# One tile shape per TensorE visit, constants as late tasks and a reorder moved from the vector engine to Pool, in a fused attention and MLP kernel

## The chip, the cores and the metric

One Trainium2 chip, one core. The metric is the device time of one execution in microseconds; a time that is quoted is the median of several executions. Engine names in the profile: PE is TensorE's matmuls, PEld its weight loads, DVE the vector engine, ACT the scalar engine, POOL is GpSimd, SP issues transfers. With one core there is no second die to compare with. The kernel before took 390.67 us (390.64 to 390.71, 3 runs). Kernels are compared only within the same rounds.

## The reference

```python
B, H, S, D = 8, 8, 576, 64                      # q, k, v: float32
q_d, k_d, v_d = (x.reshape(B, H, 144, 4, D).mean(axis=3) for x in (q, k, v))
out_up = repeat(softmax(q_d @ k_d.T / 8) @ v_d, 4)         # pooled attention, 144 x 144
mask = abs(pos[:, None] - pos[None, :]) < 4                # a narrow band
out_local = softmax(where(mask, q @ k.T / 8, -1e9)) @ v    # local attention
x = (out_up + out_local).transpose(0, 2, 1, 3).reshape(4608, 512)
h = x @ w_in                                    # 512 -> 2048
out = (h * sigmoid(h)) @ w_out                  # 2048 -> 512
```

The 64 heads are handled as 32 pairs, and two pairs make a quad (16 of them). The MLP needs x for 512 tokens at a time, so its matmuls can run from about 50 us on, between those of attention.

## The kernel before

It is one program for all engines. Tasks (a cast, a mask product, a PV visit) are put in order at build time by a scheduler that plays through estimated durations, named `cost` in nanoseconds; each engine then has its own list in that order, with waits on semaphores. A block of matmuls that TensorE runs for one task is called a visit here: S2 makes the last scores and the pooled ones, Z the row sums of the softmax, PV the product with v. The parts that the change touches (cut):

```python
def order_T(s, x):                    # q and k come back from a DMA transpose in another order
    src = (qr if x == "q" else kr)[:, :, 64 * h:64 * h + 64].rearrange("p r g -> p g r")
    dst = (qT if x == "q" else kT)[y][:, :].rearrange("p (g r) -> p g r", r=9)
    if x == "q":
        P.op("DVE", lambda e: e.tensor_reduce(dst, src.unsqueeze(3), mybir.AxisListType.X, ALU.add),
             r=[R("qr")], w=[R(f"qT{y}")], cost=745)
    else:
        P.op("ACT", lambda e: e.activation(dst, src, AF.Copy), ...)

def castv(i):                         # v summed in fours, for two pairs, on Pool; 3 buffers vd
    t = vq[0:112, :, :, 0:128]
    pool(lambda g: g.tensor_tensor(t, t, z, ALU.add), ...)
    pool(lambda g: g.tensor_tensor(vd[m][0:112, ...], x, y, ALU.add), ...)

def ph_S2(p):                         # last scores, then pooled scores: 12 matmuls of 72 columns
    ...
    for i in range(3):
        for b in range(2):
            for h in range(2):
                rows = slice(64 * h, 64 * h + 64)
                mm(D[rows, b, 120 + 72 * i:192 + 72 * i], kd[j][rows, i:i + 190:3],
                   qd[j][rows, 72 * b:72 * b + 72], ..., m="diag")

def do_mask(p):                       # DVE, both inputs in SBUF
    P.op("DVE", lambda e: e.tensor_tensor(Pt[m][:, :, :], Pt[m][:, :, :],
         mask_bf[:, :].unsqueeze(1).to_broadcast([128, 2, S_]), ALU.mult), ..., cost=800)

def ph_Z(z):                          # row sums: 32 matmuls of 128 rows, then 24 of 48 rows
    ...
        mm(D[o:o + 32, 0, 0:72], onesZ[64 * a:64 * a + 48, 8 + c // 3, :],
           Pd[m][64 * a:64 * a + 48, c // 3, c % 3, :], ..., m="diag4")

def ph_PV(p):                         # 10 matmuls of 128 rows, then 6 of 48 rows
    ...
    rows = slice(64 * a, 64 * a + 48)
    for i3 in range(3):
        for h in range(2):
            mm(D[64 * h:64 * h + 64, 1, 120:264], vd[nd][rows, i3, h, :], Pd[ms[h]][rows, :, i3, :], ..., m="diag")
```

About thirty memsets for constants stand at the head of the vector engine's list (`const_id`).

The softmax here doesn't subtract the row's maximum and nothing guards it: scores larger than these inputs give would overflow.

## Time and profile before

| what | before |
|---|---|
| median time | 390.67 us |
| TensorE busy, idle (of a span of 389.2 us) | 354.7, 34.5 us |
| TensorE idle in 0-60, 60-100, 100-260, 260-360 us | 20.3, 3.8, 6.3, 0.8 us |
| DVE, ACT, Pool busy | 239.6, 215.1, 136.9 us |

Idle time is the length of a stretch less TensorE's busy time in it. The page's line on busy time (engine, busy us, share of the span, instructions):

```profile
PE 354.7 (91%) x3841; PEld 221.3 (57%) x3880; DVE 239.6 (62%) x394; ACT 215.1 (55%) x364; POOL 136.9 (35%) x173
```

TensorE is busy nine tenths of the span; the DVE, at 62%, has room on average.

### The profile page before, as it was taken

What the parts mean: (1) busy time and instruction counts of PE and PEld (TensorE: products, weight loads), DVE (VectorE), ACT (ScalarE), POOL (GpSimd) and SP (SyncE); (2) the same over time, 40 slices, a digit from 0 to 9 for tenths busy, and PEclk for the clock granted to TensorE, in tenths of its full rate; (3) what the DMA queues carried; (4) which work ended last, traced back from release to release, by engine and by line L of the source; (5) the groups of instructions that cost most, each with busy time, mean ns of one, the idle gap of its engine ahead of it and who ended that gap; (6) DMA issues with size and microseconds to landing.
All of it is one profiled execution on the core that took longest, in us unless ns stands there. A gap on an engine that the chain in (4) does not pass through costs nothing.

```text
span 389.2 us, 9061 instructions
## 1 busy us (share of the span) xinstructions
PE 354.7 (91%) x3841; PEld 221.3 (57%) x3880; DVE 239.6 (62%) x394; ACT 215.1 (55%) x364; POOL 136.9 (35%) x173
## 2 busy tenths in 40 slices
PE   0768599898999999999699999999999999999996
PEld 0656476655655556556455655666555656556542
DVE  6927477779978775986558899654363433334310
ACT  4756367666656765786167768463424344344321
POOL 7746826377624533452534622550040000000000
PEclk9968699999999999999879999999999999999999
DMA  8998997699999999999999999964000101101012
GB/s 260 323 319 232 177 250 191 193 250 240 262 247 274 194 252 242 285 219 220 173 256 239 195 174 226 211 156 108 27 29 32 51 27 44 39 27 53 29 54 81
DMA packets 87464, 66.77 MB, mean 172 GB/s; under 512 B 65152, under 2 KB 67200, under 8 KB 87424
## 3 DMA queue, kind: packets, MB, share of 16 engines
q1 hardware_dynamic: 83200, 59.90, 66.1%
q0 software_dynamic: 4224, 6.29, 7.3%
q8 instruction: 30, 0.49, 0.6%
q14 instruction: 10, 0.08, 0.1%
HBM read 53.67 MB, written 9.88 MB: 163 GB/s over the span
## 4 chain that ended last, share of the span: by engine, by line
PE 76%; DVE 15%; DMA 5%; issue 3%; ACT 1%; DVEq 0%; ACTq 0%
PE hps L481 31%; PE ops L481 30%; PE duo L481 12%; DMA qr<-qb 5%; DVE qd L519 3%; DVE qT L388 3%; DVE gT L754 2%; DVE qT L499 2%; DVE Pt L556 2%; PE duo L491 1%; DVE kd L519 1%; PE ops L491 0%; DVE rr L577 0%; DVE osb L308 0%; DVE duo L655 0%
## 5 line engine op out<-in xcount | busy, mean ns | idle before, releaser
L481 PE MATMUL hps<-xT,w_in_sb 128*128 128x512 f32 x544 | 169.9, 437 | 4.1 <-DVE gT L754 3.9
L754 DVE SCALAR_TENSOR_TENSOR gT<-th,hps 128x512 bf16<-128x512 f32 x136 | 92.5, 682 | 87.6 <-ACT th L752 87.5
L481 PE MATMUL ops<-w_out_bf,gT 128*128 128x512 bf16 x537 | 137.6, 383 | 3.9 <-issue 2.4
L752 ACT ACTIVATE th<-hps 128x512 f32<-128x512 f32 x136 | 81.2, 598 | 107.5 <-PE hps L481 107.3
L481 PEld LDWEIGHTS hps<-xT,w_in_sb 128*128 128x128 f32 x544 | 101.3, 193 | 34.5 <-DVE gT L754 7.1
L481 PEld LDWEIGHTS ops<-w_out_bf,gT 128*128 128x128 bf16 x576 | 47.5, 98 | 68.3 <-issue 25.5
L731 POOL TENSOR_TENSOR xT<-xo 128x576 fp32r<-128x576 f32 (+2 forms) x40 | 39.9, 1018 | 73.1 <-DVE xo L714 73.0
L433 POOL TENSOR_TENSOR vq<-vq 112x768 f32<-112x768 f32 x12 | 22.4, 1868 | 37.4 <-DMA vq<-in_v_dram 37.4
L556 DVE TENSOR_TENSOR Pt<-Pt,mask_bf 128x1152 bf16<-128x1152 bf16 x32 | 28.1, 884 | 11.8 <-ACT Pt L548 11.7
L775 ACT ACTIVATE osb<-ops 128x512 f32<-128x512 f32 x36 | 21.5, 597 | 25.1 <-PE ops L481 24.9
L532 ACT ACTIVATE Pt<-duo 128x912 bf16<-128x912 f32 x28 | 26.0, 928 | 6.4 <-PE duo L481 6.3
L519 DVE TENSOR_REDUCE qd<-qT 128x144 bf16<-128x576 bf16 x32 | 24.1, 752 | 5.7 <-PE duo L481 4.5
L422 POOL CAST qb<-qs 128x576 bf16<-128x576 f32 x27 | 18.8, 705 | 22.9 <-PE duo L491 17.8
L427 ACT ACTIVATE vb<-vs 128x640 bf16<-128x640 f32 x30 | 21.8, 738 | 4.0 <-DMA vs<-in_v_dram 2.4
L422 POOL CAST kb<-ks 128x576 bf16<-128x576 f32 x27 | 18.8, 708 | 8.4 <-DMA kr<-kb 6.6
L711 DVE TENSOR_TENSOR xo<-duo,Rb 128x456 f32<-128x456 f32 x29 | 18.0, 628 | 5.0 <-PE duo L481 2.9
L388 DVE TENSOR_REDUCE qT<-qr 128x576 bf16<-128x576 bf16 x16 | 18.6, 1162 | 3.4 <-DMA qr<-qb 3.4
L519 DVE TENSOR_REDUCE kd<-kT 128x144 bf16<-128x576 bf16 x26 | 18.9, 741 | 1.3 <-ACT kT L391 1.3
L391 ACT ACTIVATE kT<-kr 128x576 bf16<-128x576 bf16 x16 | 19.1, 1221 | 0.1
L550 ACT ACTIVATE Pd<-duo 128x432 bf16<-128x432 f32 x30 | 16.0, 534 | 0.0
L481 PE MATMUL duo<-qd,kd 64*64 64x72 bf16 x360 | 14.2, 218 | 0.8 <-DVE kd L519 0.8
L481 PEld LDWEIGHTS duo<-qT,kT 64*128 64x128 bf16 x284 | 8.1, 95 | 11.9 <-issue 6.3
(119 smaller groups left out, 297.6 us busy)
## 6 DMA issues: line engine op xcount, KB each, us to landing
vs<-in_v_dram SPq DMA_DIRECT2D x60, 160.0 KB, 5.2
out_dram<-osb SPq DMA_DIRECT2D x36, 256.0 KB, 2.0
Rb<-scr SPq DMA_DIRECT2D x24, 360.0 KB, 6.8
qs<-in_q_dram SPq DMA_DIRECT2D x29, 288.0 KB, 6.2
ks<-in_k_dram SPq DMA_DIRECT2D x29, 288.0 KB, 6.2
vq<-in_v_dram SPq DMA_DIRECT2D x24, 288.0 KB, 6.3
w_in_sb<-in_moe_w_in_dram POOLq DMA_DIRECT2D x4, 1024.0 KB, 8.2
w_out_bf<-in_moe_w_out_dram POOLq DMA_DIRECT2D x4, 512.0 KB, 10.4
```

What stands on the lines that cost most here:

```text
L388: P.op("DVE", lambda e: e.tensor_reduce(dst, src.unsqueeze(3), mybir.AxisListType.X, ALU.add), r=[R("qr")], w=[R(f"qT{y}")], cost=745)
L422: pool(lambda g: g.tensor_copy(dst, t), r=rs_, w=w, cost=650)
L427: P.op("ACT", lambda e: e.activation(vb[m][:, :, :], t, AF.Copy), r=rs_, w=[R(f"vb{m}")], cost=730)
L433: pool(lambda g: g.tensor_tensor(t, t, z, ALU.add), r=[R("vq"), R("vqz")], w=[R("vq")], cost=1900)
L481: return P.op("PE", lambda t: t.matmul(out_, lhsT, rhs, start=start, stop=stop, skip_group_check=True), r, w, cost=cost)
L519: P.op("DVE", lambda e: e.tensor_reduce(dst[j][:, 0:144], src[y][:, :].rearrange("p (g r) -> p g r", r=4), mybir.AxisListType.X, ALU.add), ...
L532: later("ACT", f"e1{p}", [(lambda e: e.activation(Pt[m][:, :, 0:456], D[:, :, 0:456], AF.Exp, scale=0.125), bk, [R(f"P{m}")], 930)], bk)
L556: P.op("DVE", lambda e: e.tensor_tensor(Pt[m][:, :, :], Pt[m][:, :, :], mask_bf[:, :].unsqueeze(1).to_broadcast([128, 2, S_]), ALU.mult), ...
L731: P.op("POOL", lambda e, dst=dst, in0=in0, in1=in1: e.tensor_tensor(dst, in0, in1, ALU.add), r=[R(f"xo{x}")], w=xblk(kc, t, e_), cost=200 ...
L752: later("ACT", f"th{n}", [(lambda e: e.activation(th[tb][:, :], hp, AF.Tanh, scale=0.5), [hr], [R(f"th{tb}")], 597)], [hr], pre=[f"st{n - ...
L754: later("DVE", f"st{n}", [(lambda e: e.scalar_tensor_tensor(gT[j % 2][:, f, :], th[tb][:, :], 1.0, hp, ALU.add, ALU.mult), [hr, R(f"th{tb} ...
L775: later("ACT", f"ob{n}", [(lambda e: e.activation(osb[s_][:, :], ops[:, ob, :], AF.Copy, scale=0.5), [R(f"o{ob}", True)], [R(f"osb{s_}")], ...
```

## The change

The intent: within a visit, matmuls on 48 rows follow matmuls on 128 rows, and each such change of tile shape costs time: in the trace of the kernel before, 146 ns from the last pair of one shape to the first of the next in PV, where full-height pairs follow each other every 49 ns, and 128 ns in Z, where single matmuls follow every 8 on average. So the v means and the sum weights are padded with zeros to 128 rows (PV, Z). The pooled scores use 144 columns where they can (S2). The constants become tasks that may run late. The q reorder goes from the DVE to Pool. To feed the padded v means, half of the second v sum goes from Pool to the DVE (`castv1`). Quad 7 gets its q and k through the DMA transpose too. Some estimated durations are mended, and the order of all tasks is searched anew. The core of the diff (cut):

```diff
-        vd = sb("vd", [128, 3, 2, 64], BF16, NVD)             # NVD = 3
+        vd = sb("vd", [128, 2, 3, 2, 64], BF16, NVD)          # NVD = 2, zero outside its rows
...
             if x == "q":
-                P.op("DVE", lambda e: e.tensor_reduce(dst, src.unsqueeze(3), mybir.AxisListType.X, ALU.add),
-                     r=[R("qr")], w=[R(f"qT{y}")], cost=745)
+                pool(lambda e: e.tensor_copy(dst, src), r=[R("qr")], w=[R(f"qT{y}")], cost=700)
...
-            pool(lambda g: g.tensor_tensor(vd[m][0:112, :, :, :].rearrange("p i h d -> p h i d"), x, y, ALU.add),
-                 r=[R("vq")], w=[R(f"vd{m}")], cost=1100)
+            pool(lambda g: g.tensor_tensor(
+                vd[m][0:48, 0, :, :, :].rearrange("p i h d -> p h i d"), x[0:48], y[0:48], ALU.add), ..., cost=1030)
+
+        def castv1(i):
+            x, y = (vq[64:112, :, :, lo:lo + 64] for lo in (0, 64))
+            P.op("DVE", lambda e: e.tensor_tensor(
+                vd[m][64:112, 1, :, :, :].rearrange("p i h d -> p h i d"), x, y, ALU.add), ..., cost=480)
...
-            for i in range(3):
-                for b in range(2):
-                    for h in range(2):
-                        mm(D[rows, b, 120 + 72 * i:192 + 72 * i], kd[j][rows, i:i + 190:3], qd[j][rows, 72 * b:72 * b + 72], ...
+            for i, b, lo, hi in ((0, 0, 0, 144), (1, 1, 0, 144), (2, 0, 0, 72), (2, 1, 72, 144)):
+                for h in range(2):
+                        mm(D[rows, b, x:x + hi - lo], kd[j][rows, i:i + 190:3], qd[j][rows, lo:hi], ...
...
-                    mm(D[o:o + 32, 0, 0:72], onesZ[64 * a:64 * a + 48, 8 + c // 3, :], ..., m="diag4")
+                    mm(D[o:o + 32, 0, 0:72], onesZ[:, 8 + 2 * a + y, :], rhs, ..., m="col4")
...
-                    mm(D[64 * h:64 * h + 64, 1, 120:264], vd[nd][rows, i3, h, :], Pd[ms[h]][rows, :, i3, :], ..., m="diag")
+                    mm(D[64 * h:64 * h + 64, 1, 120:264], vd[nd][:, a, i3, h, :], t[:, i3, 0:144] ..., m="col")
...
-        const_sel()                                            # and some thirty memsets at the head of the DVE's list
+        task("DVE", "c.ones", [], const_ones)                  # likewise c.dm, c.pad, c.vd
```

## The prediction

> **What bounds the kernel now.** I read the page first (busy shares, slices, chain), then the stretches table, then the timeline of single visits on TensorE. The page:
>
> ```profile
> PE   0768599898999999999699999999999999999996
> DVE  6927477779978775986558899654363433334310
> PEclk9968699999999999999879999999999999999999
> DMA  8998997699999999999999999964000101101012
> PE 76%; DVE 15%; DMA 5%; issue 3%; ACT 1%; DVEq 0%; ACTq 0%
> ```
>
> A slice is 9.7 us. TensorE (PE) is at nine tenths or more from slice 8 on, with one hole in slice 19. Loading keeps the DMA engines full for about 25 slices, then only the MLP is left, at the full rate of PE. The chain that ended last is three quarters PE. The stretches (columns: stretch, its us, then busy us of PE, PEld, DVE, ACT, POOL, granted clock, DMA share, GB/s):
>
> ```profile
> 0.00:60.00 60.00, 39.73 (x860) 31.70 (x862) 38.28 (x90) 33.98 (x60) 37.01 (x68) 0.86 1.03 261
> 60.00:100.00 40.00, 36.15 (x547) 24.02 (x550) 32.93 (x49) 27.99 (x52) 23.79 (x27) 1.00 0.85 223
> 100.00:180.00 80.00, 77.91 (x970) 47.03 (x977) 63.82 (x99) 53.32 (x89) 34.37 (x41) 1.00 1.09 247
> 180.00:200.00 20.00, 16.78 (x151) 10.06 (x149) 11.03 (x16) 10.13 (x17) 8.63 (x9) 0.83 1.26 181
> 200.00:260.00 60.00, 59.00 (x682) 36.30 (x690) 47.05 (x74) 41.31 (x68) 27.84 (x27) 1.00 1.03 213
> 260.00:360.00 100.00, 99.21 (x537) 59.21 (x546) 41.58 (x64) 40.56 (x69) 5.24 (x5) 1.00 0.13 44
> ```
>
> PE idles 20.3 us in the first 60 us (8.85 of it before its first matmul), 3.9 in the next 40, 6.3 in 100 to 260, and 0.8 of 100 after that. DMA saturation does not bind the end: at 260 us, when loading is over, about 100 us of MLP still wait for PE, so PE always has a backlog and every microsecond of PE time removed after some 60 us should leave the total. The DVE (63.8 of 80 us in the middle) is the runner-up.
>
> **Where PE loses time.** One attention visit after another in the timeline, clock 1.00:
>
> ```profile
> 153.18 0.44 PE L481 MATMUL duo<-Pt,vb 128*64 128x120 bf16 x10
> 153.86 0.44 PE L481 MATMUL duo<-Pt,vb 128*64 128x120 bf16 x10
> 154.54 1.20 PE L481 MATMUL hps<-xT,w_in_sb 128*128 128x512 f32 x4
> ...
> 155.67 0.58 PE L481 MATMUL duo<-qT,kT 64*128 64x120 bf16 x10
> 156.18 0.46 PE L481 MATMUL duo<-qd,kd 64*64 64x72 bf16 x12
> ```
>
> A PV visit takes 0.68 us from start to start. The starts of its single records give the parts: the ten full-height matmuls go in pairs every 49 ns, the six 48-row ones of 144 columns every 60 ns, so streaming is 5 x 49 + 3 x 60 = 425 ns. The other 255 ns are two changes of tile shape: from the last pair of one shape to the first of the next it is 146 to 152 ns instead of 49 to 60, and the first pair after it is followed 25 to 27 ns late. One change costs about 0.12 us.
>
> [...] In S2 the pooled scores reload the same weights for every 72 columns: 253 ns between the first and last of 12 starts, 23 ns each or 46 a pair, against 30 ns by columns (a 144-column pair takes 60). [...] Here the DVE's reordering reduce takes 1162 ns, Pool's cast of as many elements 705:
>
> ```profile
> L388 DVE TENSOR_REDUCE qT<-qr 128x576 bf16<-128x576 bf16 x16 | 18.6, 1162 | 3.4 <-DMA qr<-qb 3.4
> L422 POOL CAST qb<-qs 128x576 bf16<-128x576 f32 x27 | 18.8, 705 | 22.9 <-PE duo L491 17.8
> ```
>
> **The change part by part.**
> 1. PV in one shape: 32 visits lose their inner change, 32 x 0.12 = 3.8 us. Where two PV follow each other directly (9 times after 60 us, some 11 in all), the change between them goes too: 11 x 0.12 = 1.3 us. Sum 5.1 us. Streaming stays 60 ns a pair.
> 2. Z in one shape: 12 visits, 128 ns instead of 8 at the boundary: 12 x 0.12 = 1.4 us. Its 56 matmuls keep their 8 ns each.
> 3. S2: the change from scores to pooled scores stays (142 ns), but 12 matmuls become 4 of 144 columns and 4 of 72. Pairs: 2 x 60 + 2 x 46 = 212 ns, before 6 x 46 = 276. 32 x 0.064 = 2.0 us.
> 4. Quad 7 goes from PE transposes to the DMA transpose: two visits of nine less, each about 0.51 us (457 ns between first and last start, plus one step): 1.0 us. It adds two transposes to a full DMA, hidden if they are issued in time.
> So PE work falls by 5.1 + 1.4 + 2.0 + 1.0 = 9.5 us. Of the 1 to 3 parts, 26 of 32 PV and S2 visits and all Z lie after 60 us: about 26 x 0.12 + 9 x 0.12 + 1.4 + 26 x 0.064 = 7.3, plus the 1.0 makes 8.3 us on the path. The rest falls in a stretch where PE waits anyway; I count none of it.
> 5. Constants as late tasks. PE starts at 8.85 us, released by the second q cast on the DVE, which runs both casts from 7.39 because some 30 memsets stand ahead. The second k pair only arrives at 7.46, so the load is the next bound: PE can start perhaps 0.7 to 1 us earlier. Counted 0.8.
> 6. q reordered on Pool: DVE loses 16 x 1.16 = 18.6 us and two PSUM copies of 0.75, gains 12 half sums of an estimated 0.5 each = 6. Net 14 us off the DVE. Pool, busy 99 of the first 200 us, gains 18 x 0.7 = 13 us. Nothing of it lies on PE directly; it makes holes less likely.
> 7. New order of all tasks, with durations that are nearer to the trace (a DVE cast entered as 420 ns, measured 742, becomes 750). Of the 20.3 + 3.9 + 6.3 = 30.5 us of holes before 260 us I expect 2 us to go, a choice rather than a sum.
>
> Sum: 8.3 + 0.8 + 2 = 11.1, so 390.67 - 11.1 = 379.6; **I predict 379.5 us**.
>
> **Rivals.**
> A. *A new wait takes the place of the old one.* The hole at 189.7 us shows how: the DVE, working in order, waits for a DMA transpose issued at 177.1 and landed at 188.2 us, PE then waits 2.9 us for the DVE, and the clock falls (0.83 in that stretch). The Pool reorder moves the wait but the q mean behind it still stands in the DVE's order, and one more quad now takes the slow transpose. v means have two buffers instead of three, and now need Pool and then the DVE. Two more such holes cost 2 x 3 us plus some clock: 385 to 387. For it: DMA stays full. Against: the new order was chosen with better durations.
> B. *The front is the bound and stays.* If the first 60 us are set by loads (DMA share 1.03), parts 5 and 7 give nothing: about 382.
> C. *Pool becomes the bound.* 137 + 13 us within some 255 us is 59% busy; it waits in order for others (73 us for xo). A late reorder then delays scores, but the backlog of MLP covers that: at most 2 or 3 us, 382.
> D. *The new order repairs the front.* PE idles 20 us there and runs at a clock of 0.86; half of that repaired would give 370 to 374.
>
> **Range and chances.** PE savings of 7 to 9.5 us are nearly mechanical; the order may give or take 5 us. 8 in 10: 373.5 to 385.5 us. Two per cent is 382.9, within my range but 3.4 us from its middle: faster 0.76, same 0.22, slower 0.02.
>
> **What would show it.** (1, 2) No 48-row matmuls of Pd; PV from start to start about 0.55 us, in a pair 0.43 to 0.45. (3) Pooled scores 8 a visit, 190 to 220 ns. (5) First matmul near 8 us. (6) A Pool copy qT<-qr of about 0.7 us; if it takes over 1.2 us because it reads with a stride, C gains. DVE busy about 226 us. (7) PE idle before 260 us: 28 us expected; over 34 means A, under 20 means D. PE busy about 345 us. I am wrong if padded matmuls run slower than 60 ns a pair, if the end of an all-full-height visit costs more than the old end, or if holes between 100 and 260 us double.

## The result and the profile after

The changed kernel is correct and took **395.81 us** (392.50 to 396.06, 4 runs); the kernel before took 390.65 us beside it (390.38 to 390.71, 4 runs). The ratio is **1.0116**, 95% interval 1.0070 to 1.0161. A ratio here is always the mean time of one kernel's fast runs over that of the kernel before's fast runs of the same rounds, so it isn't quite the ratio of the medians. The difference counts as the same within 2%, and it points to slower. The prediction, 379.5 us in a range of 373.5 to 385.5, was wrong.

The page of the kernel after (busy times, then busy tenths in 40 slices of 9.8 us, then the shares of the chain that ended last):

```profile
PE 345.6 (88%) x3697; PEld 216.2 (55%) x3734; DVE 245.5 (63%) x376; ACT 218.2 (56%) x368; POOL 158.7 (41%) x195
PE   1475799897999998899989667999999999999996
DVE  6747677767898589567767995984373433434310
PEclk9997899898999999999999998999999999999999
...
PE 64%; DVE 16%; POOL 7%; DMA 7%; issue 3%; ACT 2%; SPq 2%; POOLq 0%; ACTq 0%; DVEq 0%
```

The profiled run took 392.50 us, the fastest of the four. TensorE has 9.1 us less work in it, 345.6 us against 354.7, as predicted. But its idle time grew from 34.5 to 45.1 us. The new weak slices are 22 to 24, counted from 0. In the chain that ended last, TensorE's share is 64% (76% before); Pool has come in with 7%, and the transfers have grown from 5 to 7%. Most of these transfers are now the loads of v for the v means (`vq`, 5% of the span), which the chain before doesn't list.

The stretches of the kernel after, with the same columns as those in the prediction:

```profile
0.00:60.00 60.00, 37.64 (x842) 29.99 (x842) 39.76 (x79) 35.62 (x64) 40.69 (x74) 0.94 1.04 269
60.00:100.00 40.00, 35.52 (x486) 24.04 (x489) 29.00 (x44) 26.50 (x50) 16.79 (x20) 0.91 0.89 217
100.00:180.00 80.00, 75.53 (x902) 45.99 (x912) 64.14 (x95) 56.08 (x91) 49.58 (x56) 1.00 1.09 245
180.00:200.00 20.00, 18.71 (x216) 11.59 (x219) 14.28 (x24) 13.91 (x24) 13.13 (x12) 1.00 1.05 251
200.00:260.00 60.00, 51.38 (x584) 31.14 (x589) 49.30 (x63) 35.93 (x60) 31.87 (x31) 0.97 0.95 186
```

TensorE's idle time (length less PE) is 22.4, 4.5, 4.5, 1.3 and 8.6 us. Between 200 and 260 us it was 1.0 us before: this stretch alone gives back 7.6 us.

The work itself is as intended. One PV visit before, then two after, in the timeline (start, us, engine and line, operation, tiles, shapes, count):

```profile
285.60 0.44 PE L481 MATMUL duo<-Pt,vb 128*64 128x120 bf16 x10
285.97 0.38 PE L481 MATMUL duo<-Pd,vd 48*64 48x144 bf16 x6
286.28 0.39 PE L481 MATMUL ops<-w_out_bf,gT 128*128 128x512 bf16 x1
```

```profile
284.34 0.44 PE L508 MATMUL duo<-Pt,vb 128*64 128x120 bf16 x10
284.62 0.35 PE L508 MATMUL duo<-Pd,vd 128*64 128x144 bf16 x6
284.80 0.42 PE L508 MATMUL duo<-Pt,vb 128*64 128x120 bf16 x10
285.06 0.35 PE L508 MATMUL duo<-Pd,vd 128*64 128x144 bf16 x6
285.34 0.50 PE L508 MATMUL hps<-xT,w_in_sb 128*128 128x512 f32 x1
```

Before, the 48-row matmuls begin 0.37 us after the first, and the next visit 0.68 us after it. After, they have 128 rows and begin 0.28 us after the first; the next visit of the same kind follows 0.46 us after it, and another kind 0.54 us after it.

Now the holes. The waits of TensorE after (what waited, for what, us in total, times, longest; `hps` and `ops` are the two products of the MLP, `gT` what it multiplies second; the first wait, 7.9 us before the first matmul, is left out):

```profile
...
PE duo L508 <- DVE Pt L582: 6.2, 3, 4.8
...
PE hps L508 <- DVE gT L782: 4.8, 4, 2.1
...
PE duo L508 <- DVE qd L546: 3.3, 2, 2.9
```

The longest of them, 4.8 us, waits for the mask product `Pt`. The timeline of Pool, the DVE and TensorE of the kernel after at that place:

```profile
229.39 1.31 POOL L453 TENSOR_TENSOR vd<-vq 48x384 bf16<-48x384 f32 x1
230.66 2.65 POOL L759 TENSOR_TENSOR xT<-xo 128x192 fp32r<-128x192 f32 x4
233.25 2.23 POOL L408 COPY qT<-qr 128x576 bf16<-128x576 bf16 x2
...
229.28 0.56 DVE L460 TENSOR_TENSOR vd<-vq 48x384 bf16<-48x384 f32 x1
229.87 6.23 DVE L582 TENSOR_TENSOR Pt<-Pt,mask_bf 128x1152 bf16<-128x1152 bf16 x1
...
236.15 0.67 PE L508 MATMUL duo<-Pt,onesZ 128*32 128x72 bf16 x32 [4.75 <-DVE Pt L582]
```

Pool works without a gap from 229.39 to 235.48 us, in seven instructions. The mask product begins at 229.87 and lasts **6.23 us**, to 236.10, that is until 0.62 us after the end of Pool's run. TensorE then stands for 4.75 us. At 214.08 us the DVE's half sum of v lasts 5.58 us in the same way, over six boundaries of Pool instructions, and TensorE waits 2.95 us for the `qd` behind it. The durations of the DVE's instructions by line in the kernel after (ns: shortest, median, longest) show which can be held up, with Pool's new copy last:

```profile
L582 DVE TENSOR_TENSOR Pt<-Pt,mask_bf x32: 747/757/6231, 14.0 to 262.6; 128x1152 bf16<-128x1152 bf16 x32
...
L460 DVE TENSOR_TENSOR vd<-vq x12: 555/623/5578, 78.1 to 261.7; 48x384 bf16<-48x384 f32 x12
...
L782 DVE SCALAR_TENSOR_TENSOR gT<-th,hps x136: 627/686/689, 51.0 to 373.5; 128x512 bf16<-128x512 f32 x136
...
L739 DVE TENSOR_TENSOR xo<-duo,Rb x31: 616/626/633, 27.4 to 289.5; 128x456 f32<-128x456 f32 x31
...
L546 DVE TENSOR_REDUCE qd<-qT x32: 694/753/754, 11.2 to 249.8; 128x144 bf16<-128x576 bf16 x32
...
L408 POOL COPY qT<-qr x18: 1138/1183/1297, 102.6 to 244.6; 128x576 bf16<-128x576 bf16 x18
```

The mask product of the kernel before:

```profile
L556 DVE TENSOR_TENSOR Pt<-Pt,mask_bf x32: 704/755/2200, 14.8 to 260.8; 128x1152 bf16<-128x1152 bf16 x32
```

Of the instructions shown, only the two with **two inputs in SBUF** (the mask product L582, up to 6231 ns for a median of 757, and the half sum L460, up to 5578 for 623) have long outliers. Those with one input in SBUF or with an input in PSUM don't stretch: their longest are 689 (L782), 633 (L739) and 754 ns (L546). Taking from each instruction the shortest of its kind, the mask products of the kernel after lose 10.3 us to this, and the half sums another 10.3 us; before, the mask products lost 5.8 us. I call this time the *excess* below. And Pool's strided copy of q takes 1183 ns where the prediction counted 700.

### The profile page after: what moved, and what is told of

It is laid out like the page before. It is cut to its first block, busy times and chain, and to the rows that moved or that the text cites.

```text
span 390.7 us, 8792 instructions
## 1 busy us (share of the span) xinstructions
PE 345.6 (88%) x3697; PEld 216.2 (55%) x3734; DVE 245.5 (63%) x376; ACT 218.2 (56%) x368; POOL 158.7 (41%) x195
## 4 chain that ended last, share of the span: by engine, by line
PE 64%; DVE 16%; POOL 7%; DMA 7%; issue 3%; ACT 2%; SPq 2%; POOLq 0%; ACTq 0%; DVEq 0%
PE hps L508 27%; PE ops L508 26%; PE duo L508 9%; DMA vq<-in_v_dram 5%; DVE Pt L582 3%; DVE qd L546 3%; DVE vd L460 3%; POOL vq L452 2%; DVE qT L526 2%; DMA qr<-qb 2%; POOL qT L408 1%; SPq L419 1%; DVE gT L782 1%; POOL xT L759 1%; DVE xo L739 1%
## 5 line engine op out<-in xcount | busy, mean ns | idle before, releaser
L782 DVE SCALAR_TENSOR_TENSOR gT<-th,hps 128x512 bf16<-128x512 f32 x136 | 92.4, 684 | 77.9 <-ACT th L780 77.6
L508 PEld LDWEIGHTS hps<-xT,w_in_sb 128*128 128x128 f32 x544 | 100.0, 190 | 35.3 <-DVE gT L782 7.6
L759 POOL TENSOR_TENSOR xT<-xo 128x576 fp32r<-128x576 f32 (+2 forms) x40 | 40.6, 1035 | 43.0 <-DVE xo L742 42.8
L582 DVE TENSOR_TENSOR Pt<-Pt,mask_bf 128x1152 bf16<-128x1152 bf16 x32 | 34.2, 1068 | 9.9 <-ACT Pt L559 5.5
L452 POOL TENSOR_TENSOR vq<-vq 112x768 f32<-112x768 f32 x12 | 22.4, 1870 | 32.4 <-DMA vq<-in_v_dram 32.4
L546 DVE TENSOR_REDUCE qd<-qT 128x144 bf16<-128x576 bf16 x32 | 23.6, 749 | 4.8 <-POOL qT L408 4.3
L410 ACT ACTIVATE kT<-kr 128x576 bf16<-128x576 bf16 x18 | 21.8, 1226 | 6.4 <-DMA kr<-kb 6.4
L441 POOL CAST kb<-ks 128x576 bf16<-128x576 f32 x27 | 18.1, 676 | 17.2 <-DMA ks<-in_k_dram 12.1
L408 POOL COPY qT<-qr 128x576 bf16<-128x576 bf16 x18 | 20.9, 1187 | 9.2 <-DMA qr<-qb 8.0
L546 DVE TENSOR_REDUCE kd<-kT 128x144 bf16<-128x576 bf16 x26 | 19.2, 746 | 8.4 <-PE duo L508 4.8
L739 DVE TENSOR_TENSOR xo<-duo,Rb 128x456 f32<-128x456 f32 x31 | 18.8, 627 | 6.4 <-PE duo L508 6.1
L460 DVE TENSOR_TENSOR vd<-vq 48x384 bf16<-48x384 f32 x12 | 16.9, 1412 | 3.0 <-POOL vq L452 2.7
L508 PE MATMUL duo<-qT,kT 64*128 64x112 bf16 (+1 forms) x280 | 13.8, 219 | 2.5 <-DVE qT L526 1.1
```

What stands on the lines that cost most here:

```text
L408: pool(lambda e: e.tensor_copy(dst, src), r=[R("qr")], w=[R(f"qT{y}")], cost=700)
L441: pool(lambda g: g.tensor_copy(dst, t), r=rs_, w=w, cost=680)
L452: pool(lambda g: g.tensor_tensor(t, t, z[0:112], ALU.add), r=[R("vq"), R("vqz")], w=[R("vq")], cost=1900)
L460: P.op("DVE", lambda e: e.tensor_tensor(vd[m][64:112, 1, :, :, :].rearrange("p i h d -> p h i d"), x, y, ALU.add), r=[R("vq"), R(f"vdz{m}" ...
L508: return P.op("PE", lambda t: t.matmul(out_, lhsT, rhs, start=start, stop=stop, skip_group_check=True), r, w, cost=cost)
L546: P.op("DVE", lambda e: e.tensor_reduce(dst[j][:, 0:144], src[y][:, :].rearrange("p (g r) -> p g r", r=4), mybir.AxisListType.X, ALU.add), ...
```

## The experiments

The theory (**T1**): the loss comes from two-input vector instructions that are held up while Pool works, because the change made Pool busier (158.7 us against 136.9) and added twelve such instructions. The rivals: the part on TensorE isn't worth what its visits say, since holes swallow it (**R1**); the new order, planned with wrong durations, is just a worse order (**R2**); Pool's slow q copy delays scores (**R3**). One rival has no run of its own: the v means have two buffers instead of three, so Pool can be held up behind PV; in the kernel after it waits 3.8 us in all for TensorE before the second v sum (8.1 in d3_again), in the kernel before not at all. "Frozen" means that the order of all tasks is written out, as found for the changed kernel or the one before, so that an edit moves nothing else. Times come from different chips; the ratios are to be compared.

| kernel | order | median us | ratio to before, 95% | excess us | PE idle us, in 0-60 / 100-260 |
|---|---|---|---|---|---|
| before (first profile) | own | 390.67 | 1 | 5.8 | 34.5, 20.3 / 6.3 |
| after (first profile) | own | 395.81 | 1.0116 (1.0070-1.0161) | 20.6 | 45.1, 22.4 / 14.4 |
| a0_after_again | after's | 391.91 | 1.0065 (1.0012-1.0119) | 19.0 | 41.5, 21.9 / 10.0 |
| a1_vsum_reduce | after's | 391.71 | 1.0023 (0.9950-1.0096) | 8.0 | 40.9, 22.7 / 11.0 |
| a2_q_on_dve | after's | 391.73 | 1.0012 (0.9947-1.0078) | 13.0 | 43.4, 21.9 / 11.7 |
| a3_both | after's | 390.15 | 0.9994 (0.9943-1.0046) | 3.3 | 41.1, 22.4 / 12.3 |
| a4_pool_waits | after's | 388.62 | 0.9993 (0.9926-1.0059) | 7.3 | 40.9, 22.2 / 10.6 |
| a6_no_holds | after's | 390.17 | 1.0002 (0.9944-1.0061) | 1.9 | 43.2, 23.4 / 12.1 |
| a5_old_shapes | after's | 400.49 | 1.0279 (1.0202-1.0355) | 23.3 | 42.8, 21.4 / 11.4 |
| b1_q_on_pool | before's | 390.93 | 1.0029 (0.9977-1.0080) | 9.8 | 32.5, 20.3 / 7.0 |
| b2_one_shape | before's | 401.73 | 1.0284 (1.0228-1.0340) | 11.9 | 45.8, 24.2 / 12.4 |
| b4_scores_sums | before's | 390.97 | 0.9945 (0.9855-1.0036) | 5.6 | 35.0, 23.0 / 5.9 |
| d1_replan_dve | new | 390.06 | 0.9971 (0.9892-1.0051) | 5.5 | 38.2, 22.1 / 9.9 |
| d2_replan_hold | new | 391.79 | 1.0062 (0.9997-1.0127) | 9.1 | 37.8, 26.7 / 6.0 |
| d3_replan_waits | new | 387.90 | 0.9910 (0.9823-0.9998) | 12.4 | 31.7, 19.9 / 5.6 |
| d3_again | as d3 | 389.07 | 0.9954 (0.9911-0.9996) | 10.4 | 39.1, 19.9 / 11.8 |
| d4_replan_free | new | 391.70 | 1.0035 (0.9982-1.0088) | 3.5 | 44.0, 24.2 / 12.0 |

The excess and the idle time are those of one profiled run each; a profile can be several us from the median, and as the shortest mask product varies from 684 to 748 ns, an excess is good to about 2 us. Six profiles (before, after, a6, a5, d3_again, d4) lack 37 to 39 of the MLP's matmul records (3697 of 3734 in the kernel after). That adds to their idle time: dropping the same records from the full profiles of a0 and b1 added 2.2 and 3.0 us.

On one core a run counts as slow when it is over 1.5% above the fastest of its kernel. Such are two of b4's runs (the profiled one among them), one each of d1's and d3's, and two of the kernel before: its first profiled run (391.0 us) and one in a later round (393.9 us). The ratios leave them out. In b4, d1 and d3 it takes one unusually fast run (385.4, 386.0, 383.2 us) to make the others slow; over all runs their ratios would be 0.9996, 0.9997 and 0.9933.

### Is the kernel after, with its order frozen, the same kernel? (a0_after_again)

The edit writes the order out; the lists of instructions are identical.

> The changed kernel itself, its order of tasks written out; the instructions of each engine are the same as before writing it out. For comparison on the same chip. Every theory: 392 to 396 us, 1.005 to 1.016 times the kernel before.

Measured: 391.91 us on another chip, ratio 1.0065; excess 19.0 us. Its worst hole, of 5.5 us, stands at 230.4 us, at the same instruction as in the first profile. So the held-up instruction is a feature of the kernel and not of one run. The two ratios (1.0116 and 1.0065) also show that a difference of half a per cent between calls means little.

### The half sum with one input (a1), the q reorder back on the DVE (a2), both (a3)

```diff
 a1: in castv1
-            P.op("DVE", lambda e: e.tensor_tensor(vd[m][64:112, 1, :, :, :]..., x, y, ALU.add), ...)
+            for h in range(2):
+                P.op("DVE", lambda e, h=h: e.tensor_reduce(
+                    vd[m][64:112, 1, :, h, :], z[:, :, h, :, :], mybir.AxisListType.X, ALU.add), ...)
 a2: in order_T
-                pool(lambda e: e.tensor_copy(dst, src), r=[R("qr")], w=[R(f"qT{y}")], cost=700)
+                P.op("DVE", lambda e: e.tensor_reduce(dst, src.unsqueeze(3), mybir.AxisListType.X, ALU.add), ...)
```

> The changed kernel with its order of tasks written out (so that nothing moves) and one edit: the v half sum on the DVE is two tensor_reduces with one SBUF input each, in place of one tensor_tensor with two SBUF inputs. Theory (a DVE instruction with two SBUF inputs waits until a run of back-to-back Pool instructions ends): the 12 half sums no longer have outliers of 3.5 and 5.6 us, all near a constant; the PE holes at 150 and 218 us go, that at 231 us (a mask product) stays; 389 to 393 us. Rival (the split of the v means over two engines, or the new order itself, makes the holes): holes stay, 395 to 397 us, since the DVE has more work.

> The changed kernel, order written out, with the q reorder back on the DVE as a tensor_reduce (one input), at the same places. Theory: Pool loses 18 instructions of 1.19 us, its runs get shorter, the sum of the excess of two-input DVE instructions over their shortest falls from about 20 us to under 10, PE idle falls by 4 to 8 us: 388 to 392 us, though the DVE has 21 us more work. Rival (the DVE's amount of work makes the holes): slower than the changed kernel, 397 to 402 us.

> Both edits together: v half sum as one-input reduces and q reorder back on the DVE. Theory: PE idle back near 36 us with PE busy 345 us, 383 to 388 us. Rival (new order makes the holes): 393 us or more.

Measured: the half sums as reduces (one input in SBUF) have no outliers left by my reading of the traces; in the timelines of b2 and d1 two of them take 1.02 to 1.03 us together. The excess falls from 19.0 us to 8.0 (a1), 13.0 (a2) and 3.3 (a3), the ratio from 1.0065 to 1.0023, 1.0012 and 0.9994. All three go the way of T1, but together they bring some 0.7%, or 2.8 us, and TensorE's idle time hardly moves (more on that under a4). In a1 a hole of 3.9 us at 232.6 remains, at the mask product, and new ones of 3.4 and 2.1 us appear at 198 and 112 us.

### Only waits added (a4_pool_waits), then all holds away (a6_no_holds)

```diff
 a4 (a6: a4 and a1 together)
         self.tag = ""
+        self.two = None
...
+        if eng == "POOL" and self.two and not dma:
+            deps.append((self.two, False))        # Pool waits for the two-input DVE instruction ahead of it in the order
...                                               # behind the half sum and behind the mask product:
+            P.two = P.streams["DVE"][-1]
```

> The changed kernel with only waits added and no work moved: each Pool compute instruction that stands behind a two-input DVE instruction (mask product or v half sum) in the planned order waits for that instruction to end. Theory (a two-input DVE instruction is held as long as Pool works back to back, and the holes of PE follow from it): the outliers of these DVE instructions shrink from up to 6 us to under 2.5, PE idle falls, and the kernel gets faster by 3 to 6 us although it only waits more: 387 to 392 us. Rival (the holes come from the order or from too much work): added waits cost, 395 to 400 us.

> The changed kernel with its order frozen, and both remedies at once: the v half sum as two one-input reduces, and Pool instructions wait for the two-input vector instruction ahead of them in the order. Theory (the held instructions are the main loss): their excess falls below 3 us in sum, and the time to 386 to 389 us, some 4 us below the changed kernel's 391.9 on an earlier chip. Rival (the held instructions are a minor part, the rest is in late transfers and a slower front): 391 us or more, as with either remedy alone.

Measured for a4, on the same chip as a0: 388.62 us, **3.3 us less**, with nothing but waits added to Pool's list. The excess fell from 19.0 to 7.3 us. The two intervals overlap (0.9926-1.0059 and 1.0012-1.0119), so the size is not sharp. The durations (ns: shortest, median, longest) of mask products and half sums, in a0 and then in a4:

```profile
L649 DVE TENSOR_TENSOR Pt<-Pt,mask_bf x32: 747/758/6246, 14.0 to 262.5; 128x1152 bf16<-128x1152 bf16 x32
L526 DVE TENSOR_TENSOR vd<-vq x12: 554/598/3352, 76.3 to 261.6; 48x384 bf16<-48x384 f32 x12
```

```profile
L653 DVE TENSOR_TENSOR Pt<-Pt,mask_bf x32: 747/758/2368, 14.0 to 259.0; 128x1152 bf16<-128x1152 bf16 x32
L529 DVE TENSOR_TENSOR vd<-vq x12: 555/630/1906, 77.2 to 258.3; 48x384 bf16<-48x384 f32 x12
```

The longest mask product fell from 6.25 to 2.37 us.

Where did the time go, if TensorE's idle time is 41.5 us in a0 and 40.9 in a4? Its busy time fell, from 349.1 to 345.9 us for the same instructions. The stretch from 60 to 260 us of both (columns as above, a0 and then a4):

```profile
60.00:260.00 200.00, 183.54 (x2207) 112.46 (x2204) 154.56 (x225) 132.54 (x221) 111.85 (x116) 0.97 0.99 222
```

```profile
60.00:260.00 200.00, 184.56 (x2242) 112.51 (x2241) 147.53 (x229) 135.34 (x227) 114.47 (x118) 1.00 1.03 227
```

The granted clock was 0.97 in a0 and 1.00 in a4. During a0's hole of 5.5 us, from 230.4 us on, the clock falls to 0.50, and it stays there from 232.9 to 239.7 us, well past the hole's end. In the profiles of the table, each of the seven holes of over 3 us after 60 us (in after, a0, a1, d1 and d3) has such a stretch of 3.4 or 6.8 us that reaches past its end; a4, without such a hole, has none between 60 and 388 us. So a long hole seems to cost more than its length, and in these two profiles most of the gain lies there. That the clock follows from the holes is read from single profiles; no run tests it.

In a6 almost nothing is held up any more:

```profile
L654 DVE TENSOR_TENSOR Pt<-Pt,mask_bf x32: 748/758/1592, 14.9 to 261.3; 128x1152 bf16<-128x1152 bf16 x32
```

But a6 took 390.17 us, ratio 1.0002. T1 had expected 386 to 389 us, the rival 391 or more; neither fits. With an excess of 1.9 us, TensorE still idles 43.2 us (some 40 without the effect of the missing records). So the held-up instructions cost about 0.6 to 0.7% of the time, some 2.5 to 3 us, and are **not** the whole loss. Each interval alone overlaps a0's, but all five kernels with fewer holds lie below it; counted from the first measurement, 1.0116, it would be 1.2%.

### Is the TensorE part worth it? (a5_old_shapes)

```diff
 a5: the old shapes, on the same lists of the other engines
-            for i, b, lo, hi in ((0, 0, 0, 144), (1, 1, 0, 144), (2, 0, 0, 72), (2, 1, 72, 144)):
+            for i, b in ((0, 0), (1, 1), (2, 0), (2, 1)):
+                for y in range(2) if i < 2 else (b,):            # 72 columns each
...
-                    mm(..., onesZ[:, 8 + 2 * a + y, :], rhs, ..., m="col4")
+                    mm(..., onesZ[rows, 8 + 2 * a + y, :], rhs[rows], ..., m="diag4")   # 48 rows; PV likewise
```

> The changed kernel, order written out, with the TensorE shapes of the kernel before put back (48-row means and sums in their own tile shape, 72-column scores); nothing else changes on any engine. If TensorE's savings count in full inside the changed kernel: 7 to 9 us slower than the changed kernel, 399 to 404 us. Rival (other engines and DMA set the pace, TensorE only waits more): within 3 us of it, 392 to 396 us.

Measured: 400.49 us, ratio 1.0279; against a0 that is 1.0279 / 1.0065 = 1.0213, or **8.3 us** (by the two intervals, some 5 to 12). The page of a5:

```profile
PE 356.5 (89%) x3823; PEld 221.9 (56%) x3862; DVE 248.5 (62%) x376; ACT 219.3 (55%) x368; POOL 160.4 (40%) x195
```

TensorE's idle time is 42.8 us, nearly a0's 41.5: the extra work lengthened the span by all of itself. This refutes R1. It also sizes the rest: all that the change does outside these shapes costs a5 2.79% over the kernel before, some 11 us net. Part of that may be a5's own: its order was searched for the new shapes, and its excess is 23.3 us.

### The parts alone in the order of the kernel before (b1, b2, b4)

```diff
 b1: in order_T
-                P.op("DVE", lambda e: e.tensor_reduce(dst, src.unsqueeze(3), mybir.AxisListType.X, ALU.add), ...)
+                pool(lambda e: e.tensor_copy(dst, src), ...)
 b2: S2, Z and PV of the kernel after, two vd buffers, half sum as in a1 (its place: right behind Pool's first sum)
 b4: S2 and Z of the kernel after, PV kept
```

> The kernel before, order written out, with only the q reorder moved from the DVE (reduce, 1.16 us) to Pool (copy, 1.19 us), at the same places. Theory: DVE work falls by 18.6 us, yet mask products are held more often: their excess over the shortest rises from 6 us to over 10; 390 to 395 us, no gain. Rival (less DVE work is a gain): 386 to 389 us.

> The kernel before with its order of tasks written out and only the TensorE parts of the change (one tile shape in PV and Z, pooled scores in 144 columns, padded v means with the second half as one-input reduces on the DVE, two v-mean buffers; four v-mean tasks come later in the order because of it). q reorder stays on the DVE, no new order, quad 7 on PE. Theory (PE savings are worth their full size where no new wait arises): PE busy about 346 us, holes as before, 382 to 385 us. Rival (the saved PE time turns into waiting because the other engines or the DMA set the pace): 389 to 391 us.

> The kernel before, order written out, with only the two TensorE parts that need nothing from Pool or DVE: pooled scores in 144-column matmuls and sums in one tile shape (padded sum weights). By the prediction's terms 32 x 0.064 + 12 x 0.12 = 3.4 us less. If PE savings count in full: 386 to 388.5 us. Rival (saved PE time turns into waiting): 390 to 392 us.

b1: 390.93 us, ratio 1.0029: no gain and no loss, though the DVE's busy time fell from 239.6 to 225.9 us. The excess of the mask products rose from 5.8 to 9.8 us. Freeing the DVE by itself bought nothing in this order; and R3 has nothing to show either, for the slow copy on Pool did no measurable harm there.

b2 is a miss: 401.73 us. I had put the half sum right behind Pool's first sum in the DVE's list, and there the DVE waits for Pool. Its timeline, with the wait in brackets:

```profile
138.06 1.03 DVE L515 TENSOR_REDUCE vd<-vq 48x192 bf16<-48x384 f32 x2 [1.88 <-POOL vq L505]
```

So b2 measures its own new waits, together with four v sums that had to move later for want of a third buffer, and says nothing of the shapes. b4: 390.97 us, ratio 0.9945 with an interval from 0.9855 to 1.0036, two of its four runs slow: inconclusive (over all four runs, 0.9996). It may contain the saving of some 3 us or not.

### A new order with true durations (d1 to d4, d3_again)

All four take 1190 or 1160 ns for the q reorder, and search the order anew.

```diff
 d1: q reorder and half sum as one-input reduces on the DVE
 d2: as after; the plan lets a two-input instruction wait for Pool (two=True), and Pool waits for it as in a4
+        if two:
+            t = max(t, self.free["POOL"])
+            self.two = op
 d3: as after, with a4's waits, no hold in the plan
-                pool(lambda e: e.tensor_copy(dst, src), r=[R("qr")], w=[R(f"qT{y}")], cost=700)
+                pool(lambda e: e.tensor_copy(dst, src), r=[R("qr")], w=[R(f"qT{y}")], cost=1190)
 d4: d2's plan, with the half sum as in a1
 d3_again: the kernel d3, five rounds
```

> The changed kernel planned anew with measured durations: q reorder (1.16 us) and v half sum as one-input reduces on the DVE, mask product 0.76 us, and a new search of the order. All TensorE parts of the change are in. Theory (the TensorE savings of 9 us are real and were lost to held DVE instructions and to an order planned with wrong durations): 380 to 386 us. Rival (the pace of the other engines and the DMA sets the end): 389 to 392 us.

> The changed kernel with its instructions as they are (q reorder on Pool, half sum with two inputs on the DVE), planned anew by a plan that knows the measured durations (Pool copy 1.19 us) and that a two-input DVE instruction starts only when Pool's run is over, with Pool waiting for it in turn. Theory: outliers of two-input instructions under 2.5 us, 382 to 387 us. Rival: 389 to 392 us.

> As the run before, but the plan knows only the true duration of the Pool copy and that Pool waits for planned two-input instructions; it does not know that these are held by a Pool run that is already going. Theory: some holds are left; between the other two and the added-waits run: 384 to 389 us. Rival: 389 to 392 us.

> The changed kernel with the v half sum as one-input reduces, q reorder on Pool with its true duration, Pool waiting for planned mask products, and a plan that knows the hold; a new search of the order. Theory: 383 to 388 us. Rival: 389 to 392 us.

> The best of the kernels so far (changed kernel, true duration of the Pool copy, Pool waits for planned two-input instructions, new search of the order), once more with more rounds. Expected 384 to 390 us, its ratio to the kernel before 0.985 to 0.998; it is faster than the kernel before if the interval stays under 1.

Measured: ratios of 0.9971, 1.0062, 0.9910 and 1.0035, and 0.9954 (0.9911 to 0.9996) in five rounds of d3. So **d3 is the best version found, half a per cent faster than the kernel before** (only just clear of 1) and 1.1% faster than the kernel after as a0 measured it. One of its runs, the first profiled one, took 383.2 us: there TensorE's holes were at the level of before (31.7 us), and the time is near what was predicted. The other profiled run, of d3_again, has more holes (39.1 us). R2 is right in part: waits and a plan with true durations got back about 4 us, of which a4's waits alone, in the order of the kernel after, had brought 3; the intervals overlap. But d2 and d4, whose plans let a two-input instruction wait for the end of Pool's run (the next section measures that this doesn't hold in general), came out no better than a0 or a4: both idle longer in front (26.7 and 24.2 us in the first 60). Each search finds another order, and these four differ by up to 1.5% on the chip.

In the five-round run, TensorE's waits and page show what remains:

```profile
PE hps L511 <- DVE gT L786: 6.2, 5, 2.0
PE ops L511 <- issue: 3.0, 10, 1.5
PE duo L511 <- issue: 2.8, 1, 2.8
...
PE 348.6 (90%) x3697; PEld 218.2 (56%) x3734; DVE 233.3 (60%) x376; ACT 216.4 (56%) x368; POOL 159.3 (41%) x195
```

These are holes of up to 2.8 us at different places, five of them before MLP matmuls that wait for `gT`, and some in which the profile shows nothing that TensorE waits for. Of the ten before `ops`, most may be missing records: the full profile of d3 has one.

### The hold by itself (m1, m2, m3)

The theory up to here said that a two-input vector instruction waits for the **end of Pool's run**. Three kernels measure it in the tail of the kernel before, where the vector engine and Pool are nearly free; only dummy instructions on buffers out of use are added, and the results stay correct.

```diff
 m2 (m3: five Pool instructions of one kind, a short memset of variable length ahead of the product)
+        def held(kind, n):
+            P.op("DVE", lambda e: e.memset(kd[0][:, 0:16], 0.0), ...)              # the marker
+            reduce(0)                                                             # 0.74 us
+            P.op("DVE", lambda e: e.tensor_tensor(Pt[0][:, :, :], Pt[1][:, :, :], Pt[2][:, :, :], ALU.mult), ...)
+            for x in range(n):                                                    # released by the marker
+                P.op("POOL", lambda e, x=x: e.tensor_copy(free[x][:, :, :], src), ...)
```

> The hold measured by itself: the kernel before, order written out, with dummy work in its last 100 us, where Pool is idle. Six tests: a DVE instruction is released by the first of n Pool copies of 576 elements that follow each other without a wait on others; n = 1, 2, 3, 5, 8 for a product with two SBUF inputs (1152 elements, 0.75 us alone), n = 5 for a reduce with one. Theory: the two-input product lasts 0.75 us for n = 1 and then about 0.7 us more for each further copy (n = 5: 3.5 us or more, n = 8: 5.5 us or more); the reduce stays at 0.75 us with n = 5. Rival (Pool and DVE [...]slow each other by a factor): the product grows to at most about twice and both kinds grow.

> The hold by itself, in the tail of the kernel before, where vector and Pool are free. In each of seven tests the vector engine runs a short marker, a one-input reduce (0.75 us) and then the tested instruction; the marker releases n Pool copies back to back (estimated 0.6 us each). Tested in order: a two-input product with n = 1, 2, 4, 6, 8; a one-input reduce with n = 8; a vector copy with n = 8. Theory (a two-input vector instruction waits for the end of the Pool run): the product lasts about 0.75 us at n = 1, and grows with n, about 0.6 us for each more copy, to 2.3 to 2.5 us at n = 4 and 4.6 to 5 us at n = 8; the reduce stays at 0.75 us. Rival ([...]the vector instruction is only slowed): the product is at most about twice its 0.75 us, and the same for n = 4, 6 and 8. The copy is open: held like the product, or not.

> As m2_hold_alone, with twelve tests: the two-input product meets a run of five Pool instructions of one kind, abutting: casts (0.6 us each), strided moves (1.17 us each, the form of the q reorder) and sums of two f32 inputs[...]; each kind with the product arriving at four moments, later by about 0.1 us each. From the traces so far: the product never starts inside a Pool instruction; at a boundary with a gap it gets in always, at an abutting boundary in about half the cases. Theory A (the kind decides): casts let it in at the first boundary (product 0.75 to 1.3 us), moves and sums at none, so it ends 0.61 us after the run's end (4 to 6 us). Theory B (the moment decides): in every kind some of the four arrivals get in at the first boundary and some do not. Theory C (neither): all twelve get in at the first boundary, so what keeps it out in the changed kernel is something that this test lacks.

m1 measured nothing: the product came to its turn only after Pool's run was over, and all five took 751 or 752 ns. In m2 and m3 it came in time. The tested products in m2, then in m3, where the second Pool instruction of a run of five strided copies is shown too:

```profile
L1005 DVE TENSOR_TENSOR Pt<-Pt x5: 771/773/774, 288.9 to 335.9; 128x1152 bf16<-128x1152 bf16 x5
```

```profile
L1004 DVE TENSOR_TENSOR Pt<-Pt x12: 696/1141/1336, 286.9 to 363.3; 128x1152 bf16<-128x1152 bf16 x12
...
294.33 1.30 DVE L1004 TENSOR_TENSOR Pt<-Pt 128x1152 bf16<-128x1152 bf16 x1
...
293.83 2.85 POOL L1010 COPY qT<-qr 128x576 bf16<-128x576 bf16 x2 [3.20 <-DVE kd L998]
```

In m2 the product took 0.77 us whether Pool ran 1, 2, 4, 6 or 8 casts. **My theory, 4.6 to 5 us at eight, is wrong.** The rival's number fits (at most twice 0.75 us, the same for every n), but its reading doesn't: the product wasn't slowed at all, and by its single record the cast that followed took 1.19 us, not 0.66, so by these numbers it stood for 0.53 us, about until the product was through. In m3, where the first strided copy had 0.68 us to go when the product began, the product lasted 1.30 us, ended 0.62 us after that copy's end, and the two copies together took 2.85 us instead of 2 x 1.17. So a two-input product and Pool's instructions **took turns by whole instructions** here. The traces of before and after fit this: all ten of their mask products of over 1 us ended 612 to 619 ns after a Pool instruction did, and all four half sums of over 1 us in the kernel after 416 to 418 ns after one. The casts of m2, expected at 0.6 us, took 0.66; three sums of m3, with a product among them, took 4.07 us. All twelve products of m3 got in at the first boundary, whatever the kind of the Pool instruction (cast, strided copy, two-input sum) and the moment of arrival. That is m3's theory C: kind and moment do not decide. The one-input reduce with eight casts stayed at 0.74 us; a vector copy took 0.48 us, while the first casts beside it took longer (2.12 us for three instead of 1.89).

With this I went through the twenty profiles (before, after and the eighteen experiments) for every two-input vector instruction that waited at least 0.2 us for a Pool instruction to end, a count of mine from single records. A recount with other cut-offs gave 132 boundaries with a gap, passed by at none, and 168 abutting ones, passed by at 78, so the counts are good to a tenth or so:

| next Pool instruction begins | boundaries | the vector instruction gets in | is passed by |
|---|---|---|---|
| after a gap (0.08 us or more) | 135 | 135 | 0 |
| before the last has ended (abutting) | 151 | 82 | 69 |

The kernel after had 19 abutting boundaries and was passed by at 15 of them, up to six times in a row (the product of 6.23 us); the kernel before had 4, and was passed by at 1. So the hold is a series of lost turns, and it grows with unbroken Pool runs. That would also explain why a4 helps: a wait makes a gap, or keeps Pool from starting. **What decides a turn at an abutting boundary stays open.** The tests of m2 and m3, where after the first no instruction of the run waits on another engine, never lost one.

## Why the prediction was wrong, point by point

Two readings in it are off, without effect on its sum: TensorE's slice 9 still shows an 8, and Pool was busy 104 of the first 200 us, not 99 (37.0 + 23.8 + 34.4 + 8.6 in its own table).

- **Parts 1 to 3 (shapes): right.** That the padded matmuls would take no longer was an estimate of mine; by single records a pair of them follows the last after 62 ns, as the pairs of 48 rows did before. The inner change of PV went from 146 to 49 ns, that of Z from 128 to 23 ns, and the pooled scores of S2 from 12 matmuls in 253 ns to 8 in 200 ns (190 to 220 predicted). a5 shows 8.3 us in the time, give or take 4; the sum of the three parts was 8.5.
- **Part 4 and TensorE's sum: right as far as can be seen.** TensorE's busy time is 345.6 us ("about 345"), but the same instructions came to 345.9 to 351.3 us in a0, a1 and a4, against 356.1 us for those of the kernel before in b1. What quad 7's part 4 alone brought was not measured.
- **Part 5: right.** The first matmul is at 7.94 us instead of 8.85 ("near 8 us"), but the first 60 us idle 22.4 us, not less than 20.3: the microsecond was lost again behind it.
- **Part 6: the step that failed.** "Nothing of it lies on PE directly; it makes holes less likely." In b1 the reorder made no measurable difference in the old order, and in the profile of after, with it, the half sum and the new order, the holes grew. Two terms were mis-sized. The Pool copy was counted as 0.7 us, read from a cast with contiguous elements; it takes 1.187 us, no less than the DVE's 1.162; that the stride is the cause, as the prediction feared, no run tested alone. The half sum was counted as 0.5 us, an estimate without a trace behind it; its shortest is 0.555 us, its mean 1.41, for it is held up. So the DVE's busy time rose to 245.5 us instead of falling to 226 (an excess of 20.6 us instead of 5.8 accounts for most of that), and Pool rose by 21.8 us instead of 13.
- **Part 7: wrong in sign.** Of the holes before 260 us, 2 us were to go; they grew from 30.4 to 41.2 us. By a5, all outside the shapes costs about 11 us together.
- **Rival A was the right one, too small and for the wrong reason.** By the prediction's own test (over 34 us of idle time before 260 us means A), A came true, and the sign it named for being wrong, holes doubled between 100 and 260 us, did too (6.3 to 14.4). But it sought the new wait in the DMA transposes and in the chain from Pool to the DVE. The two worst holes (4.75 and 2.95 us) are vector instructions that lose their turn to Pool.

The traces tell which instructions are held: 6.23 us for a mask product of 0.75 us, with two inputs in SBUF, and no stretch in 136 `gT` products with one input in PSUM (627 to 689 ns). The profile before had shown it already, with a mask product of 2.20 us for a median of 0.755. The change put 18 copies of 1.187 us, 20.9 us of work, on Pool and gave the DVE twelve more instructions with two inputs in SBUF, and the prediction had no term for it.

**What is settled and what isn't.** The shapes are worth about 8 us. The held-up instructions cost some 3 us (a3, a4 and a6 against a0, with intervals that overlap). A new plan with true durations and waits gets back about 4 us in all. What is left against the predicted 0.971 of the time before, some 2.4% at d3's 0.9954, I cannot tie to one part: the holes are spread over the front, `gT` products and late transfers, and they differ from run to run and from order to order. The loads of v and the Pool sums behind them (5% of the chain each time in after, a4, a6 and d3_again for `vq` alone) and the missing third buffer are candidates that no run tests. The wrong durations of the plan are a likely reason for the order of the kernel after, but d2 and d4 don't bear that out.

## What to carry to other kernels

Before an operation moves between the vector engine and Pool, count the vector instructions with two inputs in SBUF and ask how long Pool will run without a gap: here such an instruction, while it waited, was passed by at 69 of 151 boundaries without a gap and at none of 135 with one, and the worst took 6.23 us for 0.75. Take the moved operation's duration from the same access pattern, not from the same number of elements: here Pool's strided bf16 copy of 128x576 took 1187 ns and its contiguous cast of as many elements 675 (no run separates the stride from the types). And test a gain on one engine in a frozen order, for what else changes with it can cost more than the gain: here some 8 us of savings on TensorE met some 11 us of new losses.
